# Moving a cast off Pool, small gates for the weight loads and a third exp buffer, in the front of a linear-attention and routed-experts kernel

## The chip, the cores and the metric

One NeuronCore of a Trainium2 chip. The experiments ran in three submissions, each on another chip: e1 to e4, e5 to e8, e9 to e12. Each submission ran the kernel before beside its own runs, so between submissions compare the ratios to it rather than the times. The metric is the device time of one execution in microseconds (us). Each execution also has a span (first to last instruction), about 1.8 us shorter, and a mean granted TensorE clock. Engines: PE is TensorE (matmuls), PEld its weight loads, DVE VectorE, ACT ScalarE, POOL GpSimd, SP SyncE, which here only issues loads and stores. "SPq" is SyncE's sequencer. In the timeline lines that follow, the first two numbers are start and length in us, L281 is line 281 of the kernel, x2 the number of instructions; brackets give the idle time before, and what ended it. In a stage table the last three numbers of a row are the granted clock, the busy share of the DMA engines, and GB/s.

## The reference

```python
def _attn_ref(q, k, v):                  # each (8, 8, 576, 64), fp32
    phi = lambda x: np.where(x > 0, x, np.exp(x) - 1.0) + 1.0
    q_p, k_p = phi(q), phi(k)
    kv  = einsum('bhsd,bhse->bhde', k_p, v)
    z   = k_p.sum(axis=2)
    num = einsum('bhsd,bhde->bhse', q_p, kv)
    den = einsum('bhsd,bhd->bhs', q_p, z)[..., None] + 1e-06
    return num / den

def _moe_ref(x, w_gate, w1, w2):         # x (4608, 512), 8 experts, F 1024
    P = exp(x @ w_gate - max)            # then 8 rounds of row and column scaling (Sinkhorn)
    out = 0
    for e in range(8):
        out += P[:, e:e+1] * (maximum(x @ w1[e], 0) @ w2[e])
    return out
```

The attention output, transposed to 4608 rows of 512, is the x of the second function.

## The kernel before

The attention is worked off in 16 units (one batch, four heads each), and expert 0 is already being computed in the gaps, on the part of x (the tile `xT`) that is ready. A small planner in the kernel places every operation on an engine, with a priority and an assumed duration, and so fixes the order of instructions on each engine; on the chip each engine then ran its list in order and waited where data were missing (in the trace of before PE waits 2.2 us for a cast `vv`). Of each unit, the parts that matter here (unit `n`; cuts marked):

```python
p_in = {n: S_.pool(2) for n in "kvq"}      # two buffers each for the loaded k, v, q
p_e = S_.pool(2)                           # two buffers for exp(k), exp(q)
...
    # loads: units 2 and 3 from Pool's queue, the others from SyncE's
    (nc.gpsimd if n in (2, 3) else nc.sync).dma_start(out=gr["tile"]..., in_=AP(tensor=ten.tensor, ...))
...
    # phi(k), phi(q): exp on ACT, min on DVE, then (x + 1) max e on DVE, or the +1 on ACT
    nc.scalar.activation(out=ge["tile"], in_=gin[nm]["tile"], func=AF.Exp)
    nc.vector.tensor_scalar(out=ge["tile"], in0=ge["tile"], scalar1=1.0, scalar2=None, op0=ALU.min)
    nc.vector.scalar_tensor_tensor(out=o[:, r], in0=gin[nm]["tile"][:, r], scalar=1.0,
                                   in1=ge["tile"][:, r], op0=ALU.add, op1=ALU.max)
...
    # v: fp32 to fp16, into rows of 65 with a column of ones, on Pool
    tvv.append(fadd(("pool", 1.3), f_v, deps=[ta, tin["v"]], use=[gvv, gin["v"]], prio=pr))
    vcast[n] = tvv[0]
...
att(0, 0); att(0, 1)
w_t = {0: load_w1(0, prio=-290.0, parts=2, deps=[vcast[0]])}         # expert 0, first weights, Pool's queue
...
        if b == 1:
            w_t[0] += load_w2(0, prio=-96.5, parts=2, deps=[in_prev[0]])   # expert 0, second weights
...
w_t[1] = load_w1(1, prio=0.0, after=110.0) + load_w2(1, prio=0.0, after=115.0)
```

All weight loads go through Pool's queue; they cast fp32 to fp16 on the way (by the page, 1024 KB land for a matrix of 512x1024). Pool worked in order here: a cast of v that waits for its tile also holds back the weight loads behind it (in the trace, expert 1's loads start at 112.35 us, after the cast that began at 111.06, having waited 4.33 us for its tile). Names in the profile: `ek`, `eq` are the exponentials, `tk`, `tq` phi(k) and phi(q), `vv` the cast v, `qpT` and `xT` the transposed phi(q) and x, `num_ps`, `den_ps` numerator and denominator, `xn` their quotient, `hq`, `h`, `ye` an expert's first layer, its relu and its second layer, `w` its weights. The `deps` and `after` of the planner only fix an order; they are no waits on the chip.

The softmax here doesn't subtract the row's maximum and nothing guards it: scores larger than these inputs give would overflow.

Of the kernel before, what the change touches and what calls it, by code (L numbers as in the profile page):

```python
# [10 lines left out]
FP32 = mybir.dt.float32  # L11
FP16 = mybir.dt.float16
# [5 lines left out]
class _Plan:  # L18
# [14 lines left out]
    def add(self, eng, fn, deps=(), prio=0.0, acq=(), use=(), lat=0.0, after=0.0):  # L33

        if isinstance(eng, tuple):
            eng = {eng[0]: eng[1]}
        k = len(self.t)
        t = {"eng": eng, "fn": fn, "prio": prio, "acq": tuple(acq), "lat": lat, "kids": [], "nd": 0,
             "ready": after, "done": None, "id": k}
        self.t.append(t)  # L40
        for d in set(x for x in deps if x is not None):
            self.t[d]["kids"].append(k)
            t["nd"] += 1
        for g in list(acq) + list(use):
            g["users"].append(k)
        return k
# [76 lines left out]
def kernel(  # L123
# [10 lines left out]
    nc = tc.nc  # L134

    B, H, S, D = q.shape
# [4 lines left out]
    P = 128  # L141
    PW = 64
    NJ = S // PW
    NG = N // 512
    NTT = N // P
    NFT = F // P
    NDT = DM // P
# [3 lines left out]
    S_ = _Plan()  # L151
    add = S_.add

    const = ctx.enter_context(tc.tile_pool(name="const", bufs=1))
# [3 lines left out]
    hqp = ctx.enter_context(tc.tile_pool(name="hqp", bufs=2, space=PSUM))  # L158
# [18 lines left out]
    fp = front.enter_context(tc.tile_pool(name="fp", bufs=2))  # L177
# [1 line left out]
    kvz_t = [fp.tile([P, 2, 2, D + 1], FP16, tag=f"kvz{i}", name=f"kvz{i}", bufs=1) for i in range(2)]  # L179

    p_in = {n: S_.pool(2) for n in "kvq"}
    p_e = S_.pool(2)
    p_t = {n: S_.pool(2) for n in "kq"}
    p_vv, p_kvz, p_qpT, p_xn, p_rden = (S_.pool(2) for _ in range(5))
    p_att, p_hq, p_h = S_.pool(2), S_.pool(2), S_.pool(2)
# [6 lines left out]
    def load_w(ten, nm, pl, ap, cut, e, prio, parts=1, after=0.0, deps=()):  # L192
        g = S_.grp(pl)
        ts_ = []

        def f_al(_):
            g["tile"] = wpool.tile([P, ap[1][1], ap[2][1]], FP16, tag=nm, name=nm)
        tal = add(("none", 0.0), f_al, acq=[g], prio=prio, after=after, deps=deps)
        for i in range(parts):
            def fn(_, i=i):  # L200
                dst, a, off = g["tile"], [list(x) for x in ap], e * DM * F
                if parts > 1:
                    n = a[cut][1] // parts
                    off += i * n * a[cut][0]
                    a[cut][1] = n
                    dst = dst[:, i * n:(i + 1) * n, :] if cut == 1 else dst[:, :, i * n:(i + 1) * n]
                nc.gpsimd.dma_start(out=dst, in_=AP(tensor=ten.tensor, offset=off, ap=a))
            ti = add(("pool", 1.0), fn, use=[g], prio=prio, deps=[tal])
            ts_.append(add(("dma", 6.0 / parts), lambda _: None, deps=[ti], use=[g], prio=prio, lat=2.6))
            w_last[0] = ti  # L210
        return g, [ts_[0], ts_[-1]]

    def load_w1(e, **kw):
        return load_w(moe_w1, "w1", p_w1, [[F, P], [F * P, NDT], [1, F]], 2, e, **kw)

    def load_w2(e, **kw):
        return load_w(moe_w2, "w2", p_w2, [[DM, P], [DM * P, NFT], [1, DM]], 1, e, **kw)

    def copy(e, dst, src):
        if e == "act":  # L220
            nc.scalar.copy(out=dst, in_=src)  # L221
        elif e == "dve":
            nc.vector.tensor_copy(out=dst, in_=src)  # L223
        else:
            nc.gpsimd.tensor_copy(out=dst, in_=src)
# [1 line left out]
    w_last, in_prev = [None], [None]  # L227
    front_ids = []
    xt_done = {}
    vcast = {}  # L230

    def fadd(*a, **kw):
        t = add(*a, **kw)
        front_ids.append(t)
        return t

    def att(b, g):
        n = 2 * b + g
        pr = n - 100.0
# [7 lines left out]
        gin, tin, gt, tph = {}, {}, {}, {}  # L247
        for nm, ten in (("k", k), ("q", q), ("v", v)):
            gr = gin[nm] = S_.grp(p_in[nm])

            def fn(_, gr=gr, nm=nm, ten=ten):
# [5 lines left out]
                      deps=[w_last[0] if n in (2, 3, 4) else None, in_prev[0]])  # L257
            in_prev[0] = ti
            tin[nm] = fadd(("dma", 1.55), lambda _: None, deps=[ti], use=[gr], prio=pr, lat=2.6)
        for nm in "kq":  # L260
            ge = S_.grp(p_e)
            gt[nm] = S_.grp(p_t[nm])

            def f_e(_, ge=ge, nm=nm):
                ge["tile"] = fp.tile([P, 2, NJ, D], FP16, tag="e", name="e" + nm)
                nc.scalar.activation(out=ge["tile"], in_=gin[nm]["tile"], func=AF.Exp)

            def f_t(e, g_=gt[nm], nm=nm):
                g_["tile"] = fp.tile([P, NJ, 2, D], FP16, tag="t" + nm, name="t" + nm)
                g_["on"] = e  # L270
                if e == "act":
                    nc.scalar.add(out=g_["tile"].rearrange("p j r d -> p r j d"), in_=gin[nm]["tile"], add=1.0)  # L272

            def f_m(_, ge=ge, g_=gt[nm], nm=nm):
                nc.vector.tensor_scalar(out=ge["tile"], in0=ge["tile"], scalar1=1.0, scalar2=None, op0=ALU.min)
                o = g_["tile"].rearrange("p j r d -> p r j d")
                if g_["on"] == "act":
                    nc.vector.tensor_tensor(out=o, in0=o, in1=ge["tile"], op=ALU.max)
                else:
                    for r in range(2):  # L280
                        nc.vector.scalar_tensor_tensor(out=o[:, r], in0=gin[nm]["tile"][:, r], scalar=1.0,  # L281
                                                       in1=ge["tile"][:, r], op0=ALU.add, op1=ALU.max)
            te = fadd(("act", 1.17), f_e, deps=[tin[nm]], acq=[ge], use=[gin[nm]], prio=pr)
            tt_ = fadd({"dve": 0.6, "act": 1.17}, f_t, deps=[tin[nm]],
                       acq=[gt[nm]], use=[gin[nm]], prio=pr)
            tph[nm] = fadd(("dve", 1.35), f_m, deps=[te, tt_], use=[ge, gt[nm], gin[nm]], prio=pr)
        gvv = S_.grp(p_vv)
        tvv = []
# [3 lines left out]
        ta = fadd(("none", 0.0), f_va, deps=[tin["v"]], acq=[gvv], prio=pr)  # L292
        def f_v(e):
            copy(e, gvv["tile"][:, :, :, 0:D], gin["v"]["tile"])
        tvv.append(fadd(("pool", 1.3), f_v, deps=[ta, tin["v"]],
                        use=[gvv, gin["v"]], prio=pr))
        vcast[n] = tvv[0]
        gkv, gz = [S_.grp(p_ye[2]), S_.grp(p_ye[3])], S_.grp(p_kvz)

        def f_kv(_):  # L300
# [25 lines left out]
        for j0, j1 in ((0, 5), (5, NJ)):  # L326
# [8 lines left out]
            def f_qc(e, j0=j0, j1=j1, gp=gp):  # L335
                copy(e, gq["tile"][:, :, j0:j1, :].rearrange("p h j w -> p j h w"), gp["tile"][:, 0:j1 - j0])
            t1 = fadd(("pe", 0.06 * (j1 - j0)), f_qt, deps=[tph["q"], tqa], acq=[gp], use=[gt["q"]], prio=pr)
            tq.append(fadd({"act": 0.12 + 0.1 * (j1 - j0), "dve": 0.17 + 0.057 * (j1 - j0)}, f_qc, deps=[t1, tqa],
                           use=[gp, gq], prio=pr))
# [23 lines left out]
        for i0, i1 in ((0, 2), (2, 4), (4, 5)):  # L363
# [15 lines left out]
            t1 = fadd(("pe", 0.12 * (i1 - i0)), f_num, deps=[tden, txa], acq=[gn], use=[gq, gz], prio=pr)  # L379
            txn.append(fadd(("dve", 0.14 + 0.275 * (i1 - i0)), f_xn, deps=[t1, trd, txa], use=[gn, grd, gxn], prio=pr))  # L380
        for c2 in range(2):
# [10 lines left out]
            t1 = fadd(("pe", 0.3), f_xt, deps=txn, acq=[gx], use=[gxn], prio=pr)  # L392
# [68 lines left out]
        return add(("dve", 0.8), f_p, deps=last, prio=-200.0)  # L461

    nc.vector.memset(ones_t, 1.0)
    warm = const.tile([P, 512], FP16, tag="warm", name="warm")
    nc.vector.memset(warm, 0.0)

# [18 lines left out]
    for i in range(2):  # L485
        nc.vector.memset(vv_t[i][:, :, :, D], 1.0)
        nc.vector.memset(kvz_t[i], 0.0)
    att(0, 0)
    att(0, 1)
    w_t = {0: load_w1(0, prio=-290.0, parts=2, deps=[vcast[0]])}  # L490
    for b in range(1, B):
        att(b, 0)
        att(b, 1)
# [21 lines left out]
    prev_hq = [None]  # L515
# [4 lines left out]
    def layer1(e, g):  # L520
        gw1, tw1, gw2, tw2 = w_t[e]
        bs = range(512 * g // S, (512 * g + 511) // S + 1)
        xd_ = [xt_done[(b, c)] for b in bs for c in range(NDT)]
        th = []
        gh = S_.grp(p_h)

        def f_ha(_):
            gh["tile"] = hpool.tile([P, NFT, 512], FP16, tag="h", name="h")
        tha = add(("none", 0.0), f_ha, deps=[prev_hq[0]], acq=[gh], prio=g - 400.0)
        for f in range(NFT):  # L530
            ghq = S_.grp(p_hq)

            def f_hq(_, f=f, ghq=ghq):
                ghq["tile"] = hqp.tile([P, 512], FP32, tag="hq", name="hq")
                for c in range(NDT):
                    nc.tensor.matmul(ghq["tile"], lhsT=gw1["tile"][:, c, ts(f, P)], rhs=xT[:, c, ds(512 * g, 512)],  # L536
                                     start=(c == 0), stop=(c == NDT - 1))

            def f_rl(_, f=f, ghq=ghq):
                nc.scalar.activation(out=gh["tile"][:, f, :], in_=ghq["tile"], func=AF.Relu)  # L540
            t1 = add(("pe", 0.87), f_hq, deps=[tw1[f // 4], prev_hq[0]] + xd_, acq=[ghq], use=[gw1],
                     prio=g + 0.1 * f + 0.35)
            prev_hq[0] = t1
            x_users.append(t1)
            th.append(add(("act", 0.6), f_rl, deps=[t1, tha], use=[ghq, gh], prio=g - 400.0))
        return gh, [th, th]

# [314 lines left out]
            for tt in range(4):  # L862
                out_dma(g, tt, [fin_prev[(4 * g + tt, dh)] for dh in range(2)])

    w_t[1] = load_w1(1, prio=0.0, after=110.0) + load_w2(1, prio=0.0, after=115.0)
    xd_done, xs_prev, x_closed = {}, [None], [None]
    pe_id = {}
    for g in range(NG):
# [56 lines left out]
```

## Time and profile before

| | |
|---|---|
| time, median of 3 (range) | 981.74 us (981.48 to 982.49) |
| execution that was traced | 983.97 us, span 982.2 us |

The attention front ends near 140 us. To 192 us expert 0 is finished, then seven experts follow, all of it a nearly unbroken stream of matmuls. Where PE is this busy, time is read as the sum of its gaps: the span is the work plus the gaps. "Filler" are the matmuls on `warm`, whose results nobody uses. The lines themselves stand in the prediction below.

### The profile page before, as it was taken

The page shows a single profiled execution, that of the slowest core. Times are in us where ns is not written, and L with a number is a line of the kernel's source. Part 1 is how long each engine was busy: PE and PEld are TensorE (multiplying, and loading weights), DVE is VectorE, ACT ScalarE, POOL GpSimd, SP SyncE. Part 2 cuts the span into 40 slices and gives each one's busy share as a digit, 9 for nine tenths or more (in the row PEclk, how much of TensorE's full clock was granted, in tenths as well). Part 3 has the DMA queues.
Part 4 walks back from the last instruction along what each step waited for, and adds up shares of the span by engine and source line. Part 5 has one row for each costly group of instructions (what it writes and reads, how often), then busy time and mean ns, then how long its engine had stood idle before and what let it go on. Part 6 is the DMA issues. An engine that isn't in the chain of part 4 may idle for free.

```text
span 982.2 us, 21403 instructions
## 1 busy us (share of the span) xinstructions
PE 962.2 (98%) x8716; PEld 792.7 (81%) x8716; DVE 771.7 (79%) x1561; ACT 563.2 (57%) x1034; POOL 127.9 (13%) x171
## 2 busy tenths in 40 slices
PE   7899999999999999999999999999999999999997
PEld 4455564488888888888888888888888888888885
DVE  6898869967777777777777777777777777777774
ACT  4798754565555555555555555555555555555552
POOL 4111200001111111111111111111111111111110
PEclk9999999999999999999999999999999999999999
DMA  9886953162226312272225322272225322236663
GB/s 318 257 303 239 265 160 140 65 127 77 75 76 142 97 73 76 76 161 76 77 75 137 101 76 75 76 162 76 76 76 137 102 76 76 76 103 168 161 161 98
DMA packets 47029, 121.99 MB, mean 124 GB/s; under 512 B 4177, under 2 KB 18001, under 8 KB 46929
## 3 DMA queue, kind: packets, MB, share of 16 engines
q1 hardware_dynamic: 32128, 99.76, 30.3%
q0 software_dynamic: 14480, 20.33, 11.5%
q8 instruction: 68, 1.11, 0.5%
q10 hardware_dynamic: 320, 0.52, 0.1%
q14 instruction: 33, 0.26, 0.1%
HBM read 119.69 MB, written 17.69 MB: 140 GB/s over the span
## 4 chain that ended last, share of the span: by engine, by line
PE 89%; DVE 1%; ACT 1%; issue 0%
PE ye L809 33%; PE hq L627 23%; PE att L627 11%; PE Zye L627 6%; PE Zye L809 6%; PE ye L706 5%; PE hq L536 4%; PE xt_ps L387 0%; PE kv_ps L306 0%; PE num_ps L371 0%; PE lg_ps L405 0%; DVE tk L281 0%; PE qt_ps L332 0%; ACT tq L272 0%; PE den_ps L347 0%; ACT qpT L221 0%
## 5 line engine op out<-in xcount | busy, mean ns | idle before, releaser
L823 DVE SCALAR_TENSOR_TENSOR acc<-ye,P_sb,acc 128x256 f32<-128x256 f32 x620 | 264.9, 477 | 95.3 <-PE ye L809 77.9
L627 PEld LDWEIGHTS <-W 128*128 128x128 f16 x2016 | 197.1, 98 | 23.7
L809 PEld LDWEIGHTS <-S 128*128 128x128 f16 x1984 | 194.1, 98 | 22.7 <-issue 0.3
L809 PE MATMUL ye<-T,S 128*128 128x256 f16 x1488 | 192.8, 273 | 0.1
L833 POOL TENSOR_TENSOR acc<-acc,st 128x256 f32<-128x256 f32 x124 | 87.5, 725 | 625.6 <-ACT st L830 620.7
L653 ACT ACTIVATE h<-hq 128x512 f16<-128x512 f32 x126 | 76.3, 606 | 160.8 <-PE hq L627 160.8
L627 PEld LDWEIGHTS <-w 128*128 128x128 f16 x1512 | 147.6, 98 | 23.3 <-issue 1.0
L809 PEld LDWEIGHTS <-h 128*128 128x128 f16 x1488 | 145.6, 98 | 16.8
L627 PE MATMUL hq<-xs,W 128*128 128x256 f16 x1008 | 151.2, 273 | 0.0
L627 PE MATMUL att<-xs,W 128*128 128x256 f16 x1008 | 151.2, 272 | 0.0
L627 PE MATMUL hq<-xs,w 128*128 128x256 f16 x1008 | 140.7, 272 | 0.8 <-DVE h L656 0.8
L782 DVE TENSOR_TENSOR S<-h 128x1024 f16<-128x1024 f16 x124 | 85.4, 688 | 57.9 <-ACT h L653 57.9
L656 DVE CUSTOM_DVE_ANT_0 h<-att,s 128x512 f16<-128x512 f32 x126 | 86.7, 688 | 13.1 <-ACT s L643 13.1
L830 ACT ACTIVATE st<-Zye,P_sb 128x256 f32<-128x256 f32 x124 | 52.1, 471 | 78.0 <-PE Zye L809 78.0
L643 ACT COPY s<-hq 128x512 f32<-128x512 f32 x126 | 75.0, 595 | 36.7 <-PE hq L627 36.7
L650 ACT ACTIVATE h<-Zye 128x512 f16<-128x512 f32 x126 | 75.2, 597 | 35.1 <-PE Zye L627 35.1
L656 DVE CUSTOM_DVE_ANT_0 h<-hq,s 128x512 f16<-128x512 f32 x126 | 86.5, 686 | 0.8 <-PE hq L627 0.7
L639 ACT COPY Zye<-hq 128x512 f32<-128x512 f32 x126 | 73.3, 581 | 16.3 <-PE hq L627 16.3
L706 PE MATMUL ye<-w,h 128*128 128x512 f16 x320 | 77.6, 379 | 0.9 <-DVE acc L223 0.9
L627 PE MATMUL Zye<-xs,w 128*128 128x256 f16 x504 | 75.6, 273 | 0.0
L647 ACT COPY s<-att 128x512 f32<-128x512 f32 x126 | 74.5, 591 | 0.0
L536 PE MATMUL hq<-xT,w 128*128 128x512 f16 x288 | 70.6, 379 | 2.4 <-ACT h L540 2.2
(90 smaller groups left out, 963.1 us busy)
## 6 DMA issues: line engine op xcount, KB each, us to landing
xs<-xd SPq DMA_DIRECT2D x63, 896.0 KB, 4.6
w<-in_moe_w_dram POOLq DMA_DIRECT2D x14, 1024.0 KB, 11.7
out_dram<-acc SPq DMA_DIRECT2D x68, 128.0 KB, 2.4
kin<-in_k_dram SPq DMA_DIRECT2D x14, 576.0 KB, 6.0
qin<-in_q_dram SPq DMA_DIRECT2D x14, 576.0 KB, 5.0
vin<-in_v_dram SPq DMA_DIRECT2D x14, 576.0 KB, 6.4
xd<-xst SPq DMA_DIRECT2D x9, 512.0 KB, 2.6
xd<-xT SPq DMA_DIRECT2D x9, 256.0 KB, 7.1
```

Source lines behind the costliest of these rows:

```text
L536: nc.tensor.matmul(ghq["tile"], lhsT=gw1["tile"][:, c, ts(f, P)], rhs=xT[:, c, ds(512 * g, 512)], start=(c == 0), stop=(c == NDT - 1))
L627: nc.tensor.matmul(dst[:, p, :], lhsT=lhs(p, c), rhs=rhs(c), start=(first and p == 0 and c == 0), stop=(c == 1), skip_group_check=True)
L643: nc.scalar.copy(out=gs2["tile"], in_=gX["tile"])
L647: nc.scalar.copy(out=gs5["tile"], in_=gR["tile"])
L650: nc.scalar.activation(out=hd(0, 0), in_=Zt[1], func=AF.Relu)
L653: nc.scalar.activation(out=hd(1, 0), in_=gX["tile"], func=AF.Relu)
L656: nc.vector._custom_dve(TENSOR_ADD_SAT, out=dst, in0=ps, in1=sb, s0=3.0e38, s1=0.0)
L706: nc.tensor.matmul(gy[tt]["tile"], lhsT=gh["tile"][:, f, ds(P * tt, P)], rhs=gw2["tile"][:, f, :], start=(f == 0), stop=(f == NFT - 1))
L782: nc.vector.tensor_tensor(out=Sx[:, i], in0=a0, in1=a1, op=op)
L809: nc.tensor.matmul(bank(g_)[:, s, :], lhsT=lhs(s, kk), rhs=rhs(kk), start=(new and s == 0 and kk == 0), stop=(kk == 3), skip_group_check=True)
L823: nc.vector.scalar_tensor_tensor(out=dst(), in0=bank(g_)[:, s, :], scalar=P_sb[:, gg, e:e + 1], in1=dst(), op0=ALU.mult, op1=ALU.add)
L833: nc.gpsimd.tensor_tensor(out=dst(), in0=dst(), in1=gst["tile"], op=ALU.add)
```

## The change

Its intent: free DVE from Pool's casts, beside which its instructions took 0.55 to 0.98 us longer in eight places of the trace, and start expert 0 sooner. Without casts Pool no longer holds the weight loads back, so a small copy of a v tile is put ahead of them as a gate.

```diff
-    p_e = S_.pool(2)
+    p_e = S_.pool(3)
...
-        tvv.append(fadd(("pool", 1.3), f_v, deps=[ta, tin["v"]],
+        tvv.append(fadd(("act", 1.17) if n < 2 else ("dve", 0.75), f_v, deps=[ta, tin["v"]],
                         use=[gvv, gin["v"]], prio=pr))
-        vcast[n] = tvv[0]
+        if n in (0, 13, 15):
+            def f_gate(_):
+                nc.gpsimd.tensor_copy(out=gate, in_=gin["v"]["tile"][:, 0, 0, 0:4])
+            gates[n] = add(("pool", 0.15), f_gate, deps=[tin["v"]], use=[gin["v"]], prio=pr)
...
-    w_t = {0: load_w1(0, prio=-290.0, parts=2, deps=[vcast[0]])}
+    w_t = {0: load_w1(0, prio=-290.0, parts=2, deps=[gates[0]])}
...
+        jobs = [(f, 0, NDT) for f in range(NFT)]
+        if g == 0:     # expert 0's first two blocks in halves: the first needs only half the heads
+            jobs = [(f, c, c + 2) for c in (0, 2) for f in range(2)] + jobs[2:]
...
-    w_t[1] = load_w1(1, prio=0.0, after=110.0) + load_w2(1, prio=0.0, after=115.0)
+    w_t[1] = load_w1(1, prio=0.0, deps=[gates[13]]) + load_w2(1, prio=0.0, deps=[gates[15]])
```

More of the change, by code (lines that the diff above doesn't have):

```diff
@@ L229 @@
     xt_done = {}
-    vcast = {}
+    gates = {}
     def fadd(*a, **kw):
@@ L264, in f_e @@
             def f_e(_, ge=ge, nm=nm):
-                ge["tile"] = fp.tile([P, 2, NJ, D], FP16, tag="e", name="e" + nm)
+                ge["tile"] = fp.tile([P, 2, NJ, D], FP16, tag="e", name="e" + nm, bufs=3)
                 nc.scalar.activation(out=ge["tile"], in_=gin[nm]["tile"], func=AF.Exp)
@@ L463 @@
     nc.vector.memset(ones_t, 1.0)
+    gate = const.tile([P, 4], FP32, tag="gate", name="gate")
     warm = const.tile([P, 512], FP16, tag="warm", name="warm")
@@ L529, in layer1, with f_hq @@
         tha = add(("none", 0.0), f_ha, deps=[prev_hq[0]], acq=[gh], prio=g - 400.0)
-        for f in range(NFT):
-            ghq = S_.grp(p_hq)
-            def f_hq(_, f=f, ghq=ghq):
-                ghq["tile"] = hqp.tile([P, 512], FP32, tag="hq", name="hq")
-                for c in range(NDT):
+        ghqs = [S_.grp(p_hq) for f in range(NFT)]
+        jobs = [(f, 0, NDT) for f in range(NFT)]
+        if g == 0:
+            jobs = [(f, c, c + 2) for c in (0, 2) for f in range(2)] + jobs[2:]
+        for f, c0, c1 in jobs:
+            ghq = ghqs[f]
+            def f_hq(_, f=f, ghq=ghq, c0=c0, c1=c1):
+                if c0 == 0:
+                    ghq["tile"] = hqp.tile([P, 512], FP32, tag="hq", name="hq")
+                for c in range(c0, c1):
                     nc.tensor.matmul(ghq["tile"], lhsT=gw1["tile"][:, c, ts(f, P)], rhs=xT[:, c, ds(512 * g, 512)],
@@ L540, in f_rl @@
                 nc.scalar.activation(out=gh["tile"][:, f, :], in_=ghq["tile"], func=AF.Relu)
-            t1 = add(("pe", 0.87), f_hq, deps=[tw1[f // 4], prev_hq[0]] + xd_, acq=[ghq], use=[gw1],
+            t1 = add(("pe", 0.2175 * (c1 - c0)), f_hq, deps=[tw1[f // 4], prev_hq[0]] + xd_[0:c1 if g == 0 else None],
+                     acq=[ghq] if c0 == 0 else [], use=[gw1] + ([ghq] if c0 > 0 else []),
                      prio=g + 0.1 * f + 0.35)
@@ L544, in layer1 @@
             x_users.append(t1)
+            if c1 < NDT:
+                continue
             th.append(add(("act", 0.6), f_rl, deps=[t1, tha], use=[ghq, gh], prio=g - 400.0))
```

## The prediction

> **What bounds the kernel now.** I read the page's head first, then the stage table, then the waits of TensorE, then the timeline of the first 30 us. The head and the busy list:
>
> ```profile
> span 982.2 us, 21403 instructions
> PE 962.2 (98%) x8716; PEld 792.7 (81%) x8716; DVE 771.7 (79%) x1561; ACT 563.2 (57%) x1034; POOL 127.9 (13%) x171
> ```
>
> TensorE (PE) is busy for 962.2 of 982.2 us, so only 20.0 us of idle PE time exist, plus filler: the matmuls on `warm` that [...]compute nothing. The stage table (us, then busy time of PE, PE's weight loads, DVE, ACT, POOL) says where the 20.0 lie:
>
> ```profile
> 0.00:7.90 7.90, 5.57 (x17) 2.04 (x17) 2.85 (x9) 3.61 (x3) 0.70 (x6) 1.00 0.75 273
> 7.90:30.00 22.10, 15.89 (x171) 9.25 (x171) 18.09 (x35) 11.73 (x18) 13.09 (x15) 0.92 1.13 313
> 30.00:44.00 14.00, 13.45 (x124) 7.57 (x122) 11.08 (x23) 10.51 (x18) 2.83 (x2) 1.00 0.80 263
> 44.00:60.00 16.00, 14.87 (x205) 9.95 (x205) 15.14 (x34) 14.24 (x27) 1.81 (x2) 1.00 0.85 281
> 60.00:90.00 30.00, 27.34 (x289) 16.47 (x288) 27.43 (x54) 27.40 (x44) 5.11 (x5) 1.00 0.69 231
> 90.00:140.00 50.00, 48.78 (x592) 31.22 (x587) 39.14 (x94) 36.21 (x61) 6.59 (x6) 1.00 0.82 235
> 140.00:192.00 52.00, 52.00 (x271) 25.05 (x269) 48.42 (x135) 25.74 (x44) 0.00 (x0) 1.00 0.34 134
> ```
>
> PE idle is 2.3 + 6.2 us before 30 us, 0.55 + 1.13 + 2.66 + 1.22 = 5.6 us from 30 to 140, nothing from 140 to 192, and the remaining 5.9 after that. The change touches only the attention front, before 140 us. The filler is 11.3 us of PE busy time (34 matmuls, all before 30 us), 5.6 of it before the first data can be there. So the whole sum a change of the front could recover is 6.2 + 5.7 (filler after 7.9) + 5.6 = 17.5 us, 1.8% of the span. **Faster by over 2% is nearly excluded by that sum alone.**
>
> What PE waits for before 30 us, from the waits view of that window:
>
> ```profile
> PE qt_ps L332 <- DVE tq L281: 2.6, 2, 1.6
> PE kv_ps L306 <- POOL vv L225: 2.2, 1, 2.2
> PE hq L536 <- ACT h L540: 1.4, 1, 1.4
> ```
>
> The transposes of q wait for DVE, the first k^T v for the cast of v on Pool, expert 0 for a relu queued behind exponentials. The timeline shows why DVE is late:
>
> ```profile
> 7.92 1.15 POOL L225 CAST vv<-vin 128x1152 f16<-128x1152 f32 x1 [6.61 <-DMA vin<-in_v_dram]
> 7.94 1.43 DVE L275 TENSOR_SCALAR eq<-eq 128x1152 f16<-128x1152 f16 x1
> 12.39 1.15 POOL L225 CAST vv<-vin 128x1152 f16<-128x1152 f32 x1 [0.28 <-DMA vin<-in_v_dram]
> 12.41 2.40 DVE L281 SCALAR_TENSOR_TENSOR tk<-kin,ek 128x576 f16<-128x576 f32 x2
> 27.06 2.37 DVE L281 SCALAR_TENSOR_TENSOR tq<-qin,eq 128x576 f16<-128x576 f32 x2
> ```
>
> Undisturbed, that tensor_scalar takes 0.45 us and that pair 1.43 us elsewhere in the same timeline. Beside a Pool cast they take 0.95 to 0.98 us more.
>
> [...]the stall is nearly one whole cast (0.95 to 0.98 of 1.15 us). [...]DMA share 1.13 from 7.9 to 30 us, so a load issued earlier there need not land earlier in sum.
>
> **The change, part by part.**
> (1) *Pool casts removed.* In the DVE timeline of the front I find eight collisions: 0.98, 0.97, 0.94, 0.95, 0.88, 0.55, 0.96, 0.82 = 7.05 us of DVE time given back.
> (2) *Casts to DVE and ACT.* 14 x 0.75 = 10.5 us onto DVE, by start-to-start some 0.08 less each, and two at about 1.15 us (ACT's ops on 128x1152) onto ACT. Comparing the instruction orders, the plan also moves 4 qpT copies from DVE to ACT (2 x 0.49 + 2 x 0.42 = -1.8 us for DVE) and 2 xT copies the other way (+0.9). DVE net: 10.5 - 7.05 - 1.8 + 0.9 = +2.6 us over some 110 us. ACT net: 2 x 1.15 + 4 x 0.64 - 2 x 0.64 = +3.6 us. Both stay below PE on average, but DVE and ACT were already 91% busy from 60 to 90 us.
> (3) *Third exp buffer.* The second unit's exp of k starts at 9.46 only because of DVE's late eq ("1.91 <-DVE eq" in the timeline). Now it can follow ACT's first cast at about 9.1.
> (4) *Gates.* The first weight load is issued at 9.00 after the cast; now after a 4-column copy, about 8.1. The DMA engines are full, so I count nothing for it. The loads of expert 1 move from 112.35 to about 98 and 110 us; they are first used at 192, so nothing on the path.
> (5) *Expert 0's first two blocks split in two halves*, so that the half on the first two xT columns needs no later heads: 2 matmuls of 0.216 us = 0.4 us into a hole.
>
> Path of the first two units: eq min no longer stalled (-1.0), so tq, its transposes and qpT come 1.0 earlier. Then tk of unit 1 isn't stalled ahead of rden and xn: xn starts at about 13.7, not 15.32 (-1.6). Unit 1 follows as a whole; its two xT copies lie on DVE (0.9 us) where ACT took 1.18 with xt ready at 22.45. Expert 0 thus resumes at about 21.8, not 23.68: **-1.9**; split blocks **-0.4**. For units 2 and 3, before, exp k of unit 2 stood behind the xT copies on ACT until 23.52, although its data had landed by about 19.3; in the new order it comes ahead. Then tq of unit 2 is done at about 25.6, not 29.43, and its v cast near 26.2. PE fills 14 matmuls (about 3.1 us) from 21.8 and then waits perhaps 1.0, where it idled 1.36 + 1.55 = 2.9: **-1.9**. From 30 to 140 the greater load of DVE and ACT gives some back; I take **+1.0**, as 5.6 us of idle there are already waits for DVE and ACT and their load rises by 3%, bunched. Sum: -1.9 - 0.4 - 1.9 + 1.0 = -3.2. From 981.74: **978.5 us**.
>
> **Rivals.** (a) *DVE becomes the bound from 28 to 90 us*: it is 3.9 of 4 us busy in much of 28 to 36, and each cast now stands in its in-order queue, ahead of work PE needs (the v cast of unit 2 was ready on Pool at 24.1). For it: the 91% above. Against it: it gets back 7 us of stalls. Then the gain is eaten: 981 to 983. (b) *Weight loads of expert 1 collide with the last k, q, v loads*: brought forward to 98 us, beside a DMA share of 0.82 there, they could put units 14 and 15 back by a few us, and PE's order is fixed, so it would stall: up to +3. Against it: the loads of expert 1 already crossed the last v and xd traffic before. (c) *Everything early is hidden by DMA*: if k, q, v of unit 2 are what ends last, units 2 and 3 don't move and only -2.3 + 1.0 remains: 980.4. (d) *Better than thought*: the idle of 30 to 140 shrinks too, as no Pool stall hits DVE any more: 975.5.
>
> **Range and chances.** The middle is 978.5; (a) or (b) in part lead to 981.5, (d) to 975.3. Runs of one kernel spread 1.0 us. Over 2% is 19.6 us, above the 17.5 that exist; slower by that would need a stall nothing here shows. So 0.005 faster, 0.985 same, 0.01 slower.
>
> **What would show it.** Right: no 2.4 us pairs in DVE's timeline; DVE casts at about 0.75; first xn near 13.7; expert 0 resumed near 21.8; tq of unit 2 near 25.6; PE idle before 30 us down by about 3 to 4 (idle plus filler after 7.9, now 11.9, to about 8); 30 to 140 near 6.6; after 140 unchanged. Wrong: casts at 1.3 us[...], PE idle from 30 to 140 above 8, or v of units 14 and 15 landing late behind expert 1's weights.

Cut from it, at the marks, is what no trace or run of this case shows: that the filler does anything for the clock, a mechanism for the stalls, a reckoning of a cast on DVE, and a remark on how the DMA engines are shared. The sum: -1.9 - 0.4 - 1.9 + 1.0 = -3.2, from 981.74 to 978.5 us. The 0.75 us that it counts for a cast on DVE was my estimate; the planner assumes the same in the diff above, and the trace of the changed kernel showed 0.75 to 0.76.

## The result, and the profile after

The changed kernel took **982.68 us** (median of 4, 981.88 to 983.06), the kernel before 981.69 us beside it (median of 4, 981.48 to 982.49). A ratio here is the mean time of one kernel's fast runs over the mean of the other's fast runs of the same rounds, so not quite the ratio of these medians: 1.0007, with a 95% interval of 0.999 to 1.0025. No difference, and the time lies above the range that I had given.

The traced execution of the changed kernel was its fastest, 981.88 us. The head of its page and its busy list:

```profile
span 980.1 us, 21394 instructions
PE 962.4 (98%) x8716; PEld 791.7 (81%) x8716; DVE 772.8 (79%) x1574; ACT 566.1 (58%) x1037; POOL 111.5 (11%) x158
```

PE's busy time is the same to 0.2 us; whatever changed is in the gaps. The stage table of the changed kernel, with the columns of the one in the prediction:

```profile
0.00:7.90 7.90, 6.32 (x16) 2.15 (x16) 2.74 (x9) 3.61 (x3) 0.70 (x6) 1.00 0.73 268
7.90:30.00 22.10, 18.45 (x199) 10.62 (x200) 20.05 (x45) 16.18 (x25) 8.62 (x12) 1.00 1.11 326
30.00:44.00 14.00, 11.67 (x112) 6.86 (x110) 8.99 (x18) 9.11 (x16) 0.00 (x0) 1.00 0.84 245
44.00:60.00 16.00, 13.28 (x148) 7.32 (x146) 14.36 (x30) 14.03 (x23) 0.00 (x0) 1.00 0.88 303
60.00:90.00 30.00, 29.08 (x314) 17.66 (x312) 27.03 (x63) 26.34 (x42) 0.00 (x0) 1.00 0.64 218
90.00:140.00 50.00, 49.31 (x555) 30.95 (x556) 39.60 (x89) 37.94 (x65) 2.48 (x4) 1.00 0.82 229
140.00:192.00 52.00, 52.00 (x325) 26.13 (x323) 47.88 (x134) 26.00 (x45) 0.00 (x0) 1.00 0.37 140
```

The gaps (length less PE busy) before 30 us shrink from 8.5 to 5.2 us, and those from 60 to 140 us from 3.9 to 1.6. But from 30 to 60 us they grow from 1.7 to 5.1. DVE's timeline shows the first steps of the prediction come true: the tensor_scalar beside the old cast takes 0.45 us, the pair 1.43, and the cast 0.76:

```profile
8.05 0.45 DVE L275 TENSOR_SCALAR eq<-eq 128x1152 f16<-128x1152 f16 x1
11.90 1.43 DVE L281 SCALAR_TENSOR_TENSOR tk<-kin,ek 128x576 f16<-128x576 f32 x2
25.36 0.76 DVE L223 CAST vv<-vin 128x1152 f16<-128x1152 f32 x1
```

The waits of PE from 30 to 140 us (total, times, longest) show what is new:

```profile
PE ye L718 <- DMA w<-in_moe_w_dram: 1.9, 1, 1.9
PE num_ps L374 <- DVE xn L379: 1.4, 4, 0.4
PE qt_ps L335 <- DVE xT L223: 1.1, 1, 1.1
```

`ye` is expert 0's second layer, and it now waits for its weights. Their second half comes with Pool's second load of `w` after 17.3 us. First the kernel before, with both halves in the window, then the changed kernel, with the second half alone: the issues, and the time from issue to landing (minimum, median, maximum):

```profile
L207 POOL DMA_DIRECT2D w<-in_moe_w_dram x2: 756/762/768, 17.5 to 18.2; - x2
...
DMA to landing us min/median/max: 12.0/13.8/15.6
```

```profile
L207 POOL DMA_DIRECT2D w<-in_moe_w_dram x1: 751/751/751, 17.7 to 17.7; - x1
...
DMA to landing us min/median/max: 19.7/19.7/19.7
```

The second half, issued half a microsecond earlier, lands at 37.4 instead of 33.8 us. In between lie the loads of units 4 and 5, on SyncE's queue. The first of them, before and after:

```profile
26.72 0.37 SPq L253 DMA_DIRECT2D kin<-in_k_dram  x1
```

```profile
23.68 0.37 SPq L253 DMA_DIRECT2D kin<-in_k_dram  x1
```

It waits for a k buffer, which DVE frees at the end of unit 2's `tk`. DVE is 3 us sooner there (mainly because ACT's exp of unit 2's k now starts at 18.99 us, not at 23.52), so the load is issued 3 us sooner. It lands after 7.8 us, at 31.5. But unit 4's exp of k, which reads it, starts at 39.92 us in before and at 39.04 us here, with no wait in brackets: the sooner load serves nobody yet.

```profile
39.92 1.16 ACT L266 ACTIVATE ek<-kin 128x1152 f16<-128x1152 f32 x1
```

```profile
39.04 1.17 ACT L266 ACTIVATE ek<-kin 128x1152 f16<-128x1152 f32 x1
```

So **theory A**: the change works as intended to about 30 us; the buffers it frees sooner let the loads of units 4 and 5 compete with expert 0's second weights, which are the more urgent, and the wait for these takes the gain back. The rivals: (B) the trace of before was simply a slow execution, and there never was a gain; (C) the weights are late by their own queue; (D) the loads of units 4 and 5 are needed early; my rival (b), expert 1's weights collide with the last units.

### The profile page after: what moved, and what is told of

It reads as the page before. It is cut to its first block, busy times and chain, and to the rows that moved or that the text cites. A ratio compares the mean times of both kernels' runs of the same rounds, so it can differ in the third digit from the quotient of the medians.

```text
span 980.1 us, 21394 instructions
## 1 busy us (share of the span) xinstructions
PE 962.4 (98%) x8716; PEld 791.7 (81%) x8716; DVE 772.8 (79%) x1574; ACT 566.1 (58%) x1037; POOL 111.5 (11%) x158
## 3 DMA queue, kind: packets, MB, share of 16 engines
q0 software_dynamic: 14480, 20.33, 11.7%
q8 instruction: 68, 1.11, 0.4%
## 4 chain that ended last, share of the span: by engine, by line
PE 90%; DVE 4%; DMA 3%; ACT 2%; issue 1%; DVEq 0%; ACTq 0%
PE ye L821 33%; PE hq L639 23%; PE att L639 11%; PE Zye L639 6%; PE ye L718 6%; PE Zye L821 6%; PE hq L545 4%; DMA w<-in_moe_w_dram 3%; DVE xn L379 1%; DVE tk L281 1%; DVE tq L281 1%; PE xt_ps L390 1%; PE num_ps L374 0%; PE kv_ps L309 0%; PE qt_ps L335 0%
## 6 DMA issues: line engine op xcount, KB each, us to landing
w<-in_moe_w_dram POOLq DMA_DIRECT2D x14, 1024.0 KB, 11.7
```

## The experiments

Times are medians with their range; where a mean is used, the text says so. All kernels gave right results. Where an edit changes what the planner knows, it plans anew: by the busy lists of their pages, e4, e6, e7 and (by one operation) e11 also differ in what runs on DVE and on ACT, and not in the edited line alone.

**e1 and e2: both kernels once more, unedited.** No edit.

> The kernel before, unedited, against itself. Question: is the traced execution of before (982.2 us span, timed at 983.97) a typical one, when its unprofiled runs took 981.48 to 982.49? Theory A (my prediction was right trace to trace, but started from an untypical trace): the new spans lie near 980 (time less about 1.8), and a new trace has about 2 us less idle TensorE time before 140 us than the 14.1 us of the old one. Rival B (the old trace is typical, profiling only adds a constant): spans near 982 again, and the same waits. The ratio should be 1.000 in both.

> The changed kernel, unedited, to narrow the ratio. Both theories: 0.999 to 1.002 of before. Its trace shows whether the wait of the second layer for its weights (1.9 us at 35.6 us) is there in every execution: theory A (weights overtaken by the k, q, v loads of units 4 and 5) says between 1.5 and 3 us each time.

Measured: before, loaded anew, 983.6 us (981.93 to 985.11), against 981.84 us for the first load beside it, ratio 1.0019 (1.0005 to 1.0032). So two series of the same code differ by 0.2%. The six runs of e1 fall into two groups, 981.9 to 982.5 and 984.7 to 985.1 us; whether the new load or the single execution decides on the group, the record doesn't show. The changed kernel: 983.68 us (982.58 to 984.58), ratio 1.0017 (1.0005 to 1.0029). Before's second trace has a span of 980.2 us and 12.5 us of PE idle before 140 us, where the first had 982.2 and 14.1; the stalls of DVE beside Pool casts sum to 4.6 us in six places, against the 7.05 in eight of the first. The casts start at other times in the two traces, and so meet other DVE instructions. B is right in part: I had reckoned from a trace with more stalls than another has (e1's traced execution was the fastest of its six). The second trace of the changed kernel confirms the wait, and it is longer:

```profile
38.82 1.02 PE L718 MATMUL ye<-w,h 128*128 128x512 f16 x4 [2.67 <-DMA w<-in_moe_w_dram]
```

The waits for weights sum to 3.3 us there, a little more than the 3 that I had allowed.

**e3 and e9: hold the loads of unit 4 until the weights are there.** Everything but Pool's list stays in the order of the changed kernel.

```diff
                 gr["tile"] = fp.tile([P, 2, NJ, D], FP32, tag=nm + "in", name=nm + "in", bufs=2)
+                if n == 4 and nm == "k":
+                    nc.gpsimd.tensor_copy(out=gr["tile"][:, 0, 0, 0:4], in_=w_t[0][2]["tile"][:, NFT - 1, 0:4])
```

> The changed kernel with one 4-column Pool copy from the last rows of expert 0's second weights into the tile that the k load of unit 4 will fill, so that this load and those after it on its queue start only when these weights have landed; the order of instructions on the other engines is the same as in the changed kernel. Theory A: the weights land near 33 us, not 37.4, the wait of 1.9 us goes, and nothing is lost, because the data of units 4 and 5 aren't used before 39 us: 1.5 to 3 us faster than the changed kernel, so 979.5 to 981. Rival C (the weights are late by themselves, the queue of Pool being full): landing still near 37, no gain. Rival D (units 4 and 5 become late instead): the wait moves to the exponentials of unit 4 at 39 us, same time or slower.

> The kernel of e3 once more, built and loaded anew, because before against itself came out at 1.0019 (e1) when loaded anew. Theory A: 979.5 to 980.5 again, spread under 0.5 us[...]. Rival G (the offset of a fresh load is worth 2 us on any kernel, so the gain of e3 was luck): 981 to 983.

Measured: e3 979.94 us (979.88 to 980.08), ratio to before 0.9979 (0.9968 to 0.9991); e9, loaded anew, 979.6 us (978.96 to 980.47), 0.9971 (0.9959 to 0.9984). Against e2, e3's mean is 979.98/983.62 = 0.9963, 3.6 us less. The second half of the weights in e3, and the matmuls of the second layer that had waited:

```profile
L207 POOL DMA_DIRECT2D w<-in_moe_w_dram x1: 748/748/748, 18.1 to 18.1; - x1
...
DMA to landing us min/median/max: 14.7/14.7/14.7
```

```profile
35.67 1.03 PE L720 MATMUL ye<-w,h 128*128 128x512 f16 x4
37.22 1.17 ACT L268 ACTIVATE ek<-kin 128x1152 f16<-128x1152 f32 x1
```

There is no wait in brackets behind either: the weights land at 32.8 us, PE goes on, and the exp of unit 4 finds its k, which was asked for only at 33.11 us. PE idle from 30 to 60 us is 3.2 us, not 5.1 or 6.1, by these rows of e3's stage table:

```profile
30.00:44.00 14.00, 12.47 (x121) 7.47 (x119) 10.70 (x22) 10.62 (x18) 0.19 (x1) 1.00 0.84 273
44.00:60.00 16.00, 14.36 (x175) 8.30 (x173) 14.37 (x30) 14.12 (x25) 0.00 (x0) 1.00 0.95 338
```

PE's other waits from 30 to 60 us are the same to 0.1 us in the first trace of the changed kernel and in e3; only the 1.9 us for weights is gone. Theory A holds, C and D fall, and so does G: a fresh load gave the same. One expectation failed: e9's runs spread over 1.5 us, not under 0.5, so the hold doesn't take the spread away; what makes it isn't shown.

**e10: another way to keep them behind.** The loads of units 4 and 5 go through Pool's queue, behind the weights, with no hold.

```diff
-                (nc.gpsimd if n in (2, 3) else nc.sync).dma_start(
+                (nc.gpsimd if n in (2, 3, 4, 5) else nc.sync).dma_start(
```

> The changed kernel without the hold, but with the k, q, v loads of units 4 and 5 issued on Pool's queue, behind expert 0's second weights, not on SyncE's; the order on PE, DVE and ACT is the same. A second, independent way to keep them from overtaking. Theory A: weights land near 33 us, no PE wait for them, 979 to 981. Rival C or D: no gain over the changed kernel (982.5 to 984), or units 4 and 5 late on the slower queue.

Measured: 980.47 us (980.31 to 980.63), 0.998 (0.9967 to 0.9992). The second half of the weights landed after 14.7 us, as in e3, and PE's list of waits has no entry for weights. Two edits with nothing in common but that the loads of units 4 and 5 come behind the weights give nearly the same (e10 is 0.8 us above e9 in the mean). How the DMA engines share themselves out among the loads isn't shown, only the effect: the same half of the weights, on Pool's queue, lands 19.7 and 21.3 us after issue with SyncE's loads of units 4 and 5 beside it, and 14.2 to 14.7 us after without. (Pool's queue is called the slower one in the expectation: in the first 60 us of the changed kernel's trace, loads of k, q and v, 576 KB each, landed after medians of 9.5, 10.8 and 11.4 us from Pool's queue, and of 6.7, 6.4 and 7.5 us from SyncE's.)

**e5: the hold in the kernel before.** Here as a 4-column load on SyncE's queue, since a copy on Pool would stand ahead of casts in its list:

```diff
+                if n == 4 and nm == "k":
+                    nc.sync.dma_start(out=gd, in_=w_t[0][2]["tile"][:, NFT - 1, 0:4])
```

> The kernel before with the same hold: a tiny copy (4 columns) of expert 0's second weights stands ahead of the k load of unit 4 on its queue, so those loads start when the weights have landed. Theory A (the hold helps only where the loads of units 4 and 5 overtake the weights): in before these weights landed at 33.9 and 35.4 us in two traces, and their second half is used at 37, so there is no wait to take away: within 0.5 us of before, perhaps less spread. Rival E (the hold helps by itself, by thinning the traffic of unit 3, whatever the rest): 1.5 to 2.5 us faster than before, as e3 was.

Measured: 983.11 us (981.77 to 985.95), 1.0017 (1.0004 to 1.0029), the offset that before itself showed in e1. No gain: in before the weights came in time anyhow, so the hold helps only the changed kernel. I had expected a smaller spread; it didn't come (4.2 us). Pool casts that meet DVE at some executions and not at others may be its source; that isn't shown.

**e4 and e6: the cast of v back on Pool**, without and with the hold. The hold of e6 is the one of e5, a load on SyncE's queue, not the Pool copy of e3; e6 and e3 differ in that too.

```diff
-        tvv.append(fadd(("act", 1.17) if n < 2 else ("dve", 0.75), f_v,
+        tvv.append(fadd(("pool", 1.3), f_v,
```

> The changed kernel with the cast of v back on Pool (gates, three buffers and the split kept). If the Pool collisions cost what I reckoned: DVE pairs of 2.4 us come back, the first xn moves from 13.8 to about 15, TensorE idle plus filler between 7.9 and 30 us rises from 8.7 by 1.5 to 3 us. In the whole: 1 to 2 us slower than the changed kernel if early gains carry through; the same or faster if the end of the front is set by the wait for the second weights, which a slower start hides.

> The changed kernel with the hold and with the cast of v back on Pool. Theory A with my step 1 (Pool collisions cost DVE 7 us in the front, of which about 2 us reach the path): 2 to 4 us slower than e3, so 982 to 984; the weights no longer matter. Rival F (the cast on DVE is no gain, all gain of e3 over before is from the hold and the rest): 979.5 to 980.5.

Measured: e4 985.34 us (984.01 to 987.45), 1.0036 (1.0024 to 1.0048); e6 987.94 us (985.92 to 988.16), 1.0054 (1.0041 to 1.0068). Against e2, e4's mean is 1.9 us more, as expected; its first `xn` starts at 15.87 us, and idle plus filler from 7.9 to 30 us is 2.2 us more than in the first trace of the changed kernel, although e4 doesn't wait for weights. The means of e6 and e3 differ by 7.4 us (by the ratios to before as well), nearly twice what I had expected at most. By these ratios e6 is also some 1.8 us slower than e4 (the intervals overlap); whether the hold costs there, and why, is open. The DVE stalls sum to 9.3 us in twelve places in e6. One of them, its followers on PE, and rows of the stage table from there on:

```profile
45.46 1.30 DVE L277 TENSOR_SCALAR eq<-eq 128x1152 f16<-128x1152 f16 x1
...
47.68 0.45 PE L337 MATMUL qt_ps<-ident,tq 128*128 128x128 f16 x5 [1.76 <-DVE tq L280]
```

```profile
46.00:48.00 2.00, 0.32 (x5) 0.33 (x6) 1.85 (x3) 1.93 (x6) 0.45 (x1) 1.00 1.01 378
...
50.00:52.00 2.00, 1.87 (x58) 1.85 (x59) 1.97 (x4) 2.00 (x5) 0.70 (x1) 0.50 0.79 262
52.00:54.00 2.00, 2.00 (x19) 1.16 (x14) 1.93 (x5) 1.64 (x5) 0.46 (x1) 0.50 0.17 59
```

The stall (1.30 us where 0.45 is usual) accounts for about half of the 1.76 us that PE waits for `tq`. In this stretch PE is busy for only 0.32 of 2 us, and then the granted clock is 0.64 from 48 to 50 us, 0.50 from 50 to 54 and 0.65 from 54 to 56: four `hq` matmuls of 128x512 take 1.91 us at 52.92, and 1.02 at 56.20. The slow clock comes after the stretch full of gaps; that the gaps bring it about isn't shown. Between the traces of e6 and e3, PE idle before 140 us differs by 15.0 - 10.7 = 4.3 us, and PE's busy time by 965.4 - 961.6 = 3.8 us, mostly from slower matmuls (the granted clock before 140 us is 0.96 in e6, 1.00 in e3): together the 8.2 us between their spans. So with the cast on Pool, in the order that the planner then makes, nearly half of the cost is the slower clock. Why this order is worse than before's (985 against 982), though both cast on Pool, I didn't take apart; the clock is one difference: from 44 to 60 us it is 0.79 in the traces of e4 and e6, and 1.00 in both of before.

**e7 and e8: with the hold, undo one part.** Two exp buffers (e7), no halves in expert 0's first blocks (e8).

```diff
-    p_e = S_.pool(3)           # e7; the tile's bufs=3 goes too
+    p_e = S_.pool(2)
...
-        if g == 0:             # e8
-            jobs = [(f, c, c + 2) for c in (0, 2) for f in range(2)] + jobs[2:]
```

> The changed kernel with the hold and with two exp buffers. If the third buffer matters as I reckoned (it only lets the second unit's exp of k start some tenths earlier): 0.3 to 1 us slower than e3, so 980.3 to 981. If it carries the gain: 981.5 or more. If nothing: 979.9.

> The changed kernel with the hold and without the split of expert 0's first two blocks. My sum gave the split 0.4 us: 980.2 to 980.5. If the two matmuls only take the place of filler and PE later waits for ACT or DVE anyway: 979.9 to 980.0.

Measured: e7 981.36 us (980.63 to 982.83), 0.9997 (0.9984 to 1.0009), in the mean 1.5 us above e3, 1.9 above e9 and 2.0 above e8, more than I had given the third buffer. It is most of what the hold kernel gains: with two buffers the ratio to before is 0.9997. In e7's trace ACT's exponentials wait for a `tk` or `tq` of DVE, which frees their buffer, five times before 140 us (3.9 us in all), in e3's once (0.9 us); I had counted one wait. But the planner also moved three operations from DVE to ACT, so the buffer alone isn't shown. e8 979.67 us (978.89 to 980.05), 0.9977 (0.9964 to 0.9989), no slower than e3: the two matmuls moved ahead are worth nothing that shows.

**e11: expert 1's weights late again**, with the hold.

```diff
-    w_t[1] = load_w1(1, prio=0.0, deps=[gates[13]]) + load_w2(1, prio=0.0, deps=[gates[15]])
+    w_t[1] = load_w1(1, prio=0.0, after=110.0, deps=[gates[15]]) + load_w2(1, prio=0.0, after=115.0, deps=[gates[15]])
```

> The changed kernel with the hold, and the first weights of expert 1 loaded only after the last v tile, as the kernel before did. My rival (b) said bringing them forward to 98 us collides with units 14 and 15 and could cost up to 3 us; in the traces the last v tile lands at 117 to 120 us in the changed kernel and 111 in before. If that costs: 1 us or more faster than e3, below 979. If it lies beside PE's backlog (PE idles 0.4 us from 90 to 140 us in e3): within 0.4 us of e3.

Measured: 979.6 us (979.29 to 979.86), 0.9971 (0.9958 to 0.9983), equal to e9. My rival (b) falls as a cost: the last gate, which waits for v of unit 15, runs at 115.1 us here and at 115.0 in e9 (117.2 in e3), and PE idles only 0.3 to 0.5 us from 90 to 140 us in all three.

**e12: no gates.** The gate copies are left out; the order on PE, DVE and ACT stays.

```diff
-                nc.gpsimd.tensor_copy(out=gate, in_=gin["v"]["tile"][:, 0, 0, 0:4])
+                pass
```

> The changed kernel without the gate copies (nothing on Pool then holds the weight loads back; order on PE, DVE and ACT the same). If the gates only replace the order that the Pool casts gave, and that order matters: expert 0's first weights (2 MB read) compete with unit 0 and 1, expert 1's weights (4 MB read, some 10 us of the DMA engines by the rate of this trace) with units 4 to 6, so PE waits long before 60 us: 5 to 15 us slower than the changed kernel, 988 to 998. If the gates don't matter: 982 to 984.

Measured: 986.95 us (986.48 to 987.48), 1.0045 (1.003 to 1.0061), 3 to 4 us above the changed kernel, so below the 5 to 15 that I had expected. (The some 10 us of the DMA engines are an estimate; by the changed kernel's page, Pool's queue moved 20.33 MB in 11.7% of the engines' 980.1 us, so about 12 us for the 2.1 MB that land of expert 1.) Expert 1's weights are asked for at 22.66 us, and later PE waits 3.68 us for a relu of ACT (`h`, at 55.62 us). ACT's list has an exponential ahead of it, which had waited 3.19 us for its load of k:

```profile
53.38 1.16 ACT L266 ACTIVATE ek<-kin 128x1152 f16<-128x1152 f32 x1 [3.19 <-DMA kin<-in_k_dram]
...
56.27 3.57 PE L545 MATMUL hq<-xT,w 128*128 128x512 f16 x8 [3.68 <-ACT h L549]
```

The gates are needed, then: without them the weights come ahead of the k, q and v that are wanted first. I read them as replacing what the Pool casts did unasked.

| kernel | us, median | ratio to before | PE wait for weights in the trace |
|---|---|---|---|
| changed (first, e2) | 982.68, 983.68 | 1.0007, 1.0017 | 1.9, 3.3 us |
| before, anew (e1) | 983.6 | 1.0019 | none |
| changed + hold (e3, e9) | 979.94, 979.6 | 0.9979, 0.9971 | none |
| changed, units 4 and 5 behind (e10) | 980.47 | 0.998 | none |
| before + hold (e5) | 983.11 | 1.0017 | none |
| changed + Pool cast (e4; e6 with hold) | 985.34; 987.94 | 1.0036; 1.0054 | none |
| hold, two exp buffers (e7) | 981.36 | 0.9997 | none |
| hold, no halves (e8) | 979.67 | 0.9977 | none |
| hold, expert 1 late (e11) | 979.6 | 0.9971 | none |
| no gates (e12) | 986.95 | 1.0045 | none |

The changed kernel with the hold beats both: some 2 to 3 us under before, 0.2 to 0.3%. That is clear of noise, but far from the 2% at which a kernel counts as faster.

## Why the prediction was wrong

- **"Over 2% is nearly excluded"**: right. The bound from the sum of gaps held for every run.
- **Path of the first units**: right, most of it within some tenths. First `xn` predicted at 13.7, seen at 13.83; expert 0 resumed at 21.8, seen at 21.04; `tq` of unit 2 done at 25.6, seen at 25.4 (24.02 + 1.43); casts on DVE about 0.75, seen 0.75 to 0.76; idle plus filler from 7.9 to 30 us about 8, seen 8.5.
- **Stalls given back (1)**: right in kind. With the cast gone, 0.4 us of stalls are left in two places. But their size, 7.05 us, was one execution's; another of the same kernel had 4.6. Nor did every DVE instruction beside a Pool cast stall: `xn`, which reads PSUM, took its usual 1.28 us at 70.26 us, beside the cast at 70.33. Why some stall and others don't isn't shown.
- **The start of the sum**: the step "From 981.74" was mis-joined. The -3.2 were differences to a trace timed at 983.97. From trace to trace the change did bring 982.2 - 980.1 = 2.1 us; from the typical time to the typical time there was less to gain, as e1's trace had only 12.5 us of PE idle in the front. (Rival (d) is 975.5 where it is argued and 975.3 in the range, a slip without consequence.)
- **(4) Gates, "The DMA engines are full, so I count nothing for it"**: the step that failed, and with it the path, which has no wait for weights in it. I took from the full engines that the landing times stay as they are. But which load lands first changes. The sooner free k buffers of my own step for units 2 and 3 brought SyncE's loads forward by 3 us, into the time of the second weights, and moved these from 33.8 to 37.4 us and later. That cost 1.9 and 3.3 us of wait in two traces, and 3.6 us of time by e3 against e2. Of the 4.2 us between the predicted and the measured time this is about 2.7 (982.68 against 979.94); the other 1.4 or so lie in the start of the sum and the sizes below.
- **"From 30 to 140 I take +1.0"**: the size was right in the first trace (5.6 to 6.7 us; 7.7 in e2's) by luck, for the reason was wrong. I had put it down to the load of DVE and ACT; 1.9 us of it is the wait for weights. With that wait gone, the idle from 30 to 140 us in e3 is 4.5 us, below the 5.6 of before's first trace and equal to e1's: the load on DVE costs no more than the stalls did, and rival (a) falls.
- **Third buffer (3)** was mis-sized: a few tenths of a microsecond in my path, 1.5 to 2.0 us by e7, if the planner's new order there costs nothing. **Halves (5)**: 0.4 us reckoned, none found in e8.
- **Rival (b)** named the right kind of danger, loads brought forward that collide with others, at the wrong place. Its sign came: v of unit 15 is there at 119.1 us in the changed kernel, at 111.1 in before. But e11 shows no cost of it.

With the hold the changed kernel comes to 979.6 and 979.94 us, near the 978.5 that I had predicted without seeing that the hold was needed. Part of that nearness is luck: the start of the sum was too low for the gain reckoned from it, and the third buffer was worth more than I gave it.

## What to carry to other kernels

Work that is done sooner frees its input buffers sooner, and with them the next loads start (3 us sooner here). Where the DMA engines are as full as here (busy share 1.11 and 1.13 from 7.9 to 30 us), ask of each load brought forward whose bytes it delays, and whether anyone needs it yet; a copy of 4 columns from the urgent tile was enough here to hold the others (e3: the weights landed after 14.7 us, against 19.7 and 21.3). And before working out a gain from one trace, compare the time of that very execution with the median: two traces of the kernel before had 14.1 and 12.5 us of PE idle in the front, so one trace is one draw.

## Further measurements

- An urgent load behind others: one half of an expert's second weights on Pool's queue (0.5 MB as landed in fp16) landed 14.1 to 15.0 us after issue in the six experiments on the changed kernel (e3, e7 to e11) in which the loads of units 4 and 5 (k, q, v of 0.6 MB each) were kept behind it, and 19.7 and 21.3 us after in the two traces of the changed kernel itself, where they came in beside it on SyncE's queue.
- Two series of one kernel: before against itself came to 1.0019 (1.0005 to 1.0032), so for differences below 0.2% more rounds of one load may not do, and the kernel is better loaded anew as well.
- A tiny copy on Pool: 4 columns took 0.19 us (e3, the gate at 117.21 us) and 0.72 (changed kernel, the gate at 100.82), where the kernel's planner assumed 0.15.
